# A third V copy moved to ScalarE, an O^T copy moved to VectorE, and filler matmuls re-spread around PV and the fold

## The chip, the cores and the metric

The kernel is one program on one core of a Trainium2 chip. The metric is the device time of one execution in microseconds. A program that computes the forward value and all gradients is launched once; nothing is computed outside it.

## The reference, cut to what matters

The reference computes a block with two residual branches, its output, and the gradients of everything. The part that the change touches is the forward of branch A, a recurrent attention over 64 segments of 32 tokens:

```python
for s in range(n_seg):                       # 64 segments
    h = concat([mem, x[s*32:(s+1)*32]])      # 8 memory rows + 32 rows = 40 rows of 512
    q, k, v = h @ Wq, h @ Wk, h @ Wv         # 32 heads of 128
    p = softmax(mask(q @ k.T * scale))       # per head, 40 x 40
    o = (p @ v) @ Wo                         # 40 x 512
    mem = o[:8]                              # the next segment needs this
    outs.append(o[8:])
```

A segment cannot start before the first 8 output rows of the segment before it, so the 64 segments are a serial chain. The rest (the modulation row, the gated branch B, the backward of both) comes after it and is not touched.

## The kernel before, in words

The method `phase2` runs the 64 segments one after the other. Four segments share one tile of 128 rows of x; `s4 = s % 4` is a segment's place in its tile, and four segments in a row are called a group here. A segment's own passes take 32 of its 40 rows: the 8 of `mem` and the first 24 of x. The last 8 rows of x are known beforehand and are projected for all four segments of the next tile at once ("b rows", "tail rows"), as filler work on TensorE that is spread over the group.

The order on every engine is the order in which the code is written: `pin` chains each instruction to the one before it on its engine. Tile inserts the semaphores, and it lets two engines read one PSUM tile only one after the other. `psp` is a pool of 5 PSUM banks for nearly everything, `pst` one of 3 for the scores.

One segment, in order of TensorE:

1. K and Q projections (`proj`, line 255, four passes of 16 matmuls in four 32-column strips), each half copied out by VectorE or ScalarE into `RA`.
2. V's first chunk (`v_chunk(s, 0)`, line 650), `turns` (transposes of K and Q, line 763), V's second chunk. A V chunk uses three of the four column strips for the segment; the fourth strip carries V's tail rows for the next tile (`RBv`). Chunks are 4, 4 and 3 head groups wide (`VCH`). `self.evac("act" or "dve", ...)` picks ScalarE (line 61) or VectorE (line 63) for the copy out.
3. Scores (`st_exp`, line 773) onto a mask that was put into the score banks one segment earlier by `mask_mm` (line 717, three matmuls: 480, 480 and 360 columns), exp on ScalarE (line 775), V's third chunk.
4. PV in three parts: `den` (line 779, the row sums), `pv` (line 799), `recip` on VectorE (line 784), `ost` (scaling by 1/sum: parts 0 and 2 on VectorE, line 811; part 1 on ScalarE as four instructions, line 808). `pv(2)` and `den(2)` write the bank `or2` that the first `recip` reads, so they wait for it.
5. `ott(0..2)`: transposes of the scaled rows (line 791) and their copies to `OT`, parts 0 and 2 by ScalarE, part 1 by VectorE. `outproj` (line 223) starts with part 0.
6. The fold: `split_pair` takes the output apart into a high half (ScalarE, line 230) and a low half (VectorE, line 232), `sum_pair` adds the strips on TensorE (line 240), and ScalarE copies 8 rows into the next segment's `hT` (line 936). The next K projection waits for that copy.

Around these stand fillers: the b rows' K and Q passes under `fill(s4, "f1")` between `outproj` and the fold, their transposes under `fill(s4, "turn")`, a part of the modulation row once per group (`mod_rest`, line 200) in front of `ott(0)`, the masks of the next segment before and between the `ott`, `p1` (normalising a later tile of x), and in the last segment of a group the tail's own output projection (`tail.chunk`, line 215) in two pieces around the fold.

Of the kernel before, what the change touches and what calls it, by code (L numbers as in the profile page):

```python
# [40 lines left out]
class K:  # L41
# [395 lines left out]
    def phase2(self):  # L437
        nc, tc, cfg, io = self.nc, self.tc, self.cfg, self.io
        D, DC, H, E, L, M, T, G, NS = cfg.D, cfg.DC, cfg.H, cfg.E, cfg.L, cfg.M, cfg.T, cfg.G, cfg.NS
        GW = 128  # L440
        NP = 3
# [9 lines left out]
        with ExitStack() as ctx:  # L451
# [39 lines left out]
            NT = cfg.NT  # L491
# [45 lines left out]
            sb2 = ctx.enter_context(tc.tile_pool(name="p2s2", bufs=2))  # L537
# [17 lines left out]
            def part3(t, pi):  # L555
                return t[:, pi * PW:min((pi + 1) * PW, G * GW)].rearrange("p (g x) -> p g x", x=GW)
# [48 lines left out]
            def b_pieces(t):  # L605

                bt = btails[t] = {}
                RBt = RB

                def proj_b(x, a, n, eng):  # L610
                    hb = hxs[t][1]
                    self.col_pass(psp, Ws[x], 0, lambda c: hb[:, c, :, :].rearrange("p s q -> p (s q)"), RBt[x], eng, steps=(a, n))
                    if a + n == 8:
                        rows_out(RBt[x], DR[x], t * nseg_t, nseg_t)

                def turn_b(x):
# [12 lines left out]
                T_ = lambda x: (lambda: turn_b(x))  # L629
                return {(0, "f1"): [P("k", 0, 4, "dve"), P("k", 4, 2, "act")], (1, "f1"): [P("k", 6, 2, "dve"), P("q", 0, 4, "act")],  # L630
                        (2, "turn"): [T_("k")], (2, "f1"): [P("q", 4, 4, "dve")], (3, "turn"): [T_("q")]}

            evacs = []

# [2 lines left out]
                    evacs.pop(0)()  # L637

            first = b_pieces(0)
            first = [f for k in ((0, "f1"), (1, "f1"), (2, "f1"), (2, "turn"), (3, "turn")) for f in first[k]]  # L640
            firsts = {"k": [first[i] for i in (0, 1, 2, 5)] + [evac_turned], "q": [first[i] for i in (3, 4, 6)] + [evac_turned]}
            slots = {}

            VCH = ((0, 4), (4, 4), (8, 3))

            def v_mm(ps, j, c, lhsT, hl, a, n):

                wc = Wv[:, c, :].rearrange("p (h e) -> p h e", e=E)
                n = min(n, (H - hl + 2) // 3 - a)
                nc.tensor.matmul(ps[32 * j:32 * j + 32, 0:n * E], lhsT=lhsT, rhs=wc[:, 3 * a + hl:3 * (a + n - 1) + hl + 1:3, :],  # L650
                                 start=(c == 0), stop=(c == DC - 1), tile_position=(0, 32 * j))

            def v_evac(eng, dst, ps, a, n):

                m = n if a + n < G else n - 1
                self.evac(eng, dst[0:96, a * E:(a + m) * E], ps[0:96, 0:m * E])
                if m < n:
                    self.evac(eng, dst[0:64, (a + m) * E:(a + n) * E], ps[0:64, m * E:n * E])

            def hb_rows(t):  # L660
                return lambda c: hxs[t][1][:, c, :, :].rearrange("p s q -> p (s q)")
# [10 lines left out]
            def v_chunk(s, k):  # L672

                t, s4 = s // nseg_t, s % nseg_t
                a, n = VCH[k]
                tail_of = None
                if t + 1 < NT:
                    tail_of = (s4,) + VCH[k] if s4 < 3 and k < 2 else (k,) + VCH[2] if s4 == 3 else None
                ps = psp.tile([128, 512], F32, name="pass_ps", tag="p")
                hT = get_ht(s)  # L680
                for c in range(DC):
                    for j in range(3):
                        v_mm(ps, j, c, hT[:, c, :], j, a, n)
                    if tail_of:
                        v_mm(ps, 3, c, hb_rows(t + 1)(c), *tail_of)
                if k > 0:
                    v_evac("dve", Vsts[s % 2], ps, a, n)
                if tail_of:
                    hl, ta, tn = tail_of
                    tn = min(tn, (H - hl + 2) // 3 - ta)  # L690
                    self.evac(("act", "dve", "dve")[k], RBv[(t + 1) % 2][32 * hl:32 * hl + 32, ta * E:(ta + tn) * E],
                              ps[96:128, 0:tn * E])
                if k == 0:
                    v_evac("dve", Vsts[s % 2], ps, a, n)

            def fill(s4, where):
                for f in slots.pop((s4, where), []):
                    f()

            norms = []  # L700
            mod_r = []
            mod_at = sorted([4 * i + 4 for i in range(4 * DC - 1)] + [7])
# [10 lines left out]
            def mask_mm(pi):  # L713

                n = min(PG, G - pi * PG)
                ps = masked[pi] = pst.tile([128, PG, GW], F32, name="st_ps", tag="st")
                nc.tensor.matmul(ps[:, 0:n, 0:120], lhsT=self.ident[:, :], rhs=maskT[:, 0:n, :], start=True, stop=False,
                                 skip_group_check=True)
# [19 lines left out]
            for s in range(NS):  # L738
                s4 = s % nseg_t
                if s4 == 0:  # L740
                    if s > 0:
                        p1(s // nseg_t + P1_AHEAD, 0)
                    slots = b_pieces(s // nseg_t + 1) if s + nseg_t < NS else {}
# [50 lines left out]
                def pv(pi, or_ps=None):  # L794
                    or_ps = or_ps or ps_f32("or_ps")
                    n = min(PG, G - pi * PG)
                    for j in range(n):
                        g = pi * PG + j
                        nc.tensor.matmul(or_ps[:, j, :], lhsT=ET[:, g * GW:(g + 1) * GW], rhs=Vst[:, g * GW:(g + 1) * GW],
                                         start=True, stop=True)  # L800
                    return or_ps
# [11 lines left out]

                def ott(pi):
                    ps, n = transposes_part(Ost, pi, m=120)
                    self.evac("dve" if pi == 1 else "act", part3(OT, pi)[:, 0:n, 0:120], ps)

                def outproj():
                    ps = psp.tile([128, 256], F32, name="at_ps", tag="p")
# [67 lines left out]
                early = s4 == 0 and len(self.later) > 1  # L887
                if early:
                    self.pop_later()
                pv(2, or2)  # L890
                den(2, or2)
                recip(2, 3, or2)
                ost(2, or2, "dve")
                more = list(range(NP)) if s + 1 < NS else []
                turned = bool(slots.get((s4, "turn"))) or bool(mod_r)
                mod_row = mod_r.pop()() if mod_r else None
                if s + 1 in mod_at:
                    load, products = self.mod_rest(psp, sb2, mod_at.index(s + 1))
                    load()
                    mod_r.append(products)  # L900
                fill(s4, "turn")
                if s4 == 3:
                    turned = True
                if more and not turned:
                    mask_mm(more.pop(0))
                    mask_mm(more.pop(0))
                ott(0)
                if len(more) > 1:
                    mask_mm(more.pop(0))
                ott(1)  # L910
                if len(more) > 1:
                    mask_mm(more.pop(0))
                ott(2)
                if more:
                    mask_mm(more.pop(0))
                if not early:
                    self.pop_later()
                self.pop_later()
                nc.sync.dma_start(self.OSR[s], gl3(Ost))
                at_ps = outproj()  # L920
                evac_turned()
                if mod_row:
                    mod_row()
                if s4 < 3:
                    p1(s // nseg_t + P1_AHEAD, s4 + 1)
                if s + 1 < NS:
# [7 lines left out]
                ft = self.sum_pair(psp, parts, "at", "p")  # L934
                if hT_next is not None:
                    nc.scalar.activation(hT_next[:, :, 0:M], ft[:, :, 0:M], AF.Copy)  # L936
                if s4 == 3:
                    tail.chunk()
                tail.split()
# [14 lines left out]
            for pi in range(NP):  # L954
                ps, n = transposes_part(ET, pi)
# [4 lines left out]
            for pi in range(NP):  # L960
                ps, n = transposes_part(Vst, pi)
# [1238 lines left out]
```

## Time and profile before

| | |
|---|---|
| times of three runs | 3095.11, 3099.77, 3098.11 us; median 3098.11 us |
| the profiled execution | 3101.05 us; its span 3099.3 us; mean granted TensorE clock 0.991 |
| TensorE busy | 2981.1 us, 96% of the span |
| VectorE, ScalarE, GpSimd busy | 53%, 41%, 39% |
| DMA, mean over the span | 227 GB/s |
| the 64 segments | from 18.3 us to about 1005 us |

Four segments from the middle start (first K matmul, line 255, in the timeline) at 529.25, 544.22, 559.13 and 573.62 us, and the next one at 589.15: they take 14.97, 14.91, 14.49 and 15.53 us for s4 = 0, 1, 2, 3, together 59.90 us. In the timeline a row gives the start, the time to the last end, engine, line, operation, tiles and count, and in brackets the idle time of that engine before the row with what ended it. A matmul row's time includes the way through the array, so consecutive rows overlap; what counts for TensorE's speed is the distance between starts.

### The profile page before, as it was taken

What the parts mean: (1) busy time and instruction counts of PE and PEld (TensorE: products, weight loads), DVE (VectorE), ACT (ScalarE), POOL (GpSimd) and SP (SyncE); (2) the same over time, 40 slices, a digit from 0 to 9 for tenths busy, and PEclk for the clock granted to TensorE, in tenths of its full rate; (3) what the DMA queues carried; (4) which work ended last, traced back from release to release, by engine and by line L of the source; (5) the groups of instructions that cost most, each with busy time, mean ns of one, the idle gap of its engine ahead of it and who ended that gap; (6) DMA issues with size and microseconds to landing.
All of it is one profiled execution on the core that took longest, in us unless ns stands there. A gap on an engine that the chain in (4) does not pass through costs nothing. (4 is left out here: it accounts for less than half of the span.)

```text
span 3099.3 us, 106370 instructions
## 1 busy us (share of the span) xinstructions
PE 2981.1 (96%) x44229; PEld 1849.8 (60%) x44229; DVE 1644.9 (53%) x3874; ACT 1257.6 (41%) x3036; POOL 1215.9 (39%) x2640
## 2 busy tenths in 40 slices
PE   6999999999999799989999999999999999999999
PEld 3666666666666444445567777777777754445454
DVE  5666666666665788743255555555555542322321
ACT  2555555555554444412145555555555530111011
POOL 2454545555444222211244444444444432333322
PEclk8999999999999899999999999999999999999999
DMA  9777777777777799997689999999999998666574
GB/s 298 212 212 203 204 207 205 204 207 211 203 200 232 210 226 237 212 278 254 202 210 249 243 242 250 252 243 247 244 242 252 244 276 279 199 198 219 191 235 148
DMA packets 839319, 703.53 MB, mean 227 GB/s; under 512 B 539730, under 2 KB 711794, under 8 KB 837940
## 3 DMA queue, kind: packets, MB, share of 16 engines
q1 hardware_dynamic: 713668, 486.69, 60.5%
q0 software_dynamic: 54512, 148.63, 15.2%
q10 hardware_dynamic: 70656, 61.41, 6.3%
q8 instruction: 348, 5.70, 0.8%
q14 instruction: 135, 1.11, 0.1%
HBM read 294.93 MB, written 276.35 MB: 184 GB/s over the span
## 5 line engine op out<-in xcount | busy, mean ns | idle before, releaser
L1990 PE MATMUL gps<-rows,hrows 128*128 128x512 bf16 (+2 forms) x2160 | 417.5, 355 | 0.0
L1990 PEld LDWEIGHTS <-hrows 128*128 128x128 bf16 x2160 | 211.2, 98 | 204.6
L63 DVE CAST ot<-gps 128x512 bf16<-128x512 f32 (+3 forms) x76 | 48.2, 634 | 292.3 <-PE gps L1990 204.6
L1696 POOL COPY dOst<-RAd 96x512 bf16<-96x512 bf16 x128 | 75.4, 613 | 308.3 <-DVE RAd L63 308.3
L255 PEld LDWEIGHTS <-hT 128*32 128x32 bf16 x4096 | 117.2, 97 | 123.6 <-POOL kT L65 14.2
L650 PE MATMUL pass_ps<-Wv,hT 128*32 128x512 bf16 (+2 forms) x2304 | 186.7, 357 | 0.0
L61 ACT ACTIVATE ot<-gps 128x512 bf16<-128x512 f32 (+3 forms) x75 | 41.3, 551 | 354.3 <-PE gps L1990 208.4
L63 DVE CAST Vst<-pass_ps 96x512 bf16<-96x512 f32 (+2 forms) x256 | 126.7, 515 | 108.5 <-ACT RBv L61 92.0
L1994 POOL DMA_DIRECT2D out_dram<-ot x108 | 81.6, 755 | 254.8 <-DVE ot L63 130.6
L945 POOL TENSOR_TENSOR Pst<-Pst,rden 120x1408 bf16<-120x1408 bf16 x63 | 159.6, 2533 | 6.3 <-POOL hT L545 3.8
L255 PE MATMUL pass_ps<-Wk,hT 128*32 128x512 bf16 x2048 | 122.3, 380 | 22.6 <-ACT hT L936 15.3
L61 ACT ACTIVATE dVT<-g_ps 128x480 bf16<-128x480 f32 (+1 forms) x192 | 104.6, 545 | 96.7 <-PE g_ps L1652 96.4
L341 POOL DMA_DIRECT2D AOA<-at_rb x64 | 36.4, 568 | 259.9 <-DVE at_rb L337 259.9
L215 PE MATMUL dh_ps<-WvT,dVT 128*32 128x512 bf16 x2048 | 134.3, 382 | 0.3
L255 PE MATMUL pass_ps<-Wq,hT 128*32 128x512 bf16 x2048 | 124.1, 383 | 6.2 <-DMA Wq<-in_A_Wq_dram 6.2
L728 POOL DMA_DIRECT2D Vst<-RBv x192 | 100.4, 527 | 75.8 <-DVE RBv L63 37.0
L650 PE MATMUL pass_ps<-Wv,hb 128*32 128x512 bf16 (+2 forms) x576 | 129.6, 364 | 0.0
L2004 PE MATMUL gps5o<-WoT,rows 128*128 128x512 bf16 x592 | 128.4, 379 | 1.2 <-DMA rows<-OSR 1.2
L223 PE MATMUL at_ps<-Wo,OT 128*32 128x256 bf16 x4096 | 124.6, 274 | 4.1 <-DMA Wo<-in_A_Wo_dram 4.0
L255 PE MATMUL pass_ps<-WoT,dyT 128*32 128x256 bf16 (+1 forms) x3072 | 122.5, 308 | 0.9 <-ACT dyT L1770 0.9
L223 PE MATMUL dhq_ps<-WqT,dQT 128*32 128x256 bf16 x4096 | 122.9, 273 | 0.0
L215 PE MATMUL dh_ps<-WkT,dKT 128*32 128x512 bf16 x2048 | 122.3, 380 | 0.0
(413 smaller groups left out, 7047.9 us busy)
## 6 DMA issues: line engine op xcount, KB each, us to landing
OSR<-Ost SPq DMA_DIRECT2D x64, 352.0 KB
OT<-OT SPq DMA_DIRECT2D x64, 352.0 KB
VT<-VTr SPq DMA_DIRECT2D x64, 352.0 KB
PS<-Pst SPq DMA_DIRECT2D x64, 352.0 KB
OT_l<-OT SPq DMA_DIRECT2D x64, 352.0 KB
Pst_l<-PS SPq DMA_DIRECT2D x64, 352.0 KB
VT_l<-VT SPq DMA_DIRECT2D x64, 352.0 KB
DVR<-rows_x POOLq DMA_DIRECT2D x64, 352.0 KB, 6.2
```

Source lines behind the costliest of these rows:

```text
L61: return nc.scalar.activation(out, in_, AF.Copy)
L63: return nc.vector.tensor_copy(out, in_)
L215: self.nc.tensor.matmul(ps[32 * j:32 * j + 32, :], lhsT=lhsT, rhs=w, start=(n < 4), stop=(n >= total - 4), tile_position=(0, 32 * j))
L223: nc.tensor.matmul(ps[32 * j:32 * j + 32, :], lhsT=x[k], rhs=w[k][:, 256 * d:256 * d + 256], start=(n == 0), stop=(n == total - 1), tile_p ...
L255: self.nc.tensor.matmul(ps[32 * j:32 * j + 32, :], lhsT=lhs(c), rhs=rhs, start=(c == 0), stop=(c == DC - 1), tile_position=(0, 32 * j))
L650: nc.tensor.matmul(ps[32 * j:32 * j + 32, 0:n * E], lhsT=lhsT, rhs=wc[:, 3 * a + hl:3 * (a + n - 1) + hl + 1:3, :], start=(c == 0), stop=( ...
L728: nc.gpsimd.dma_start(Vst[96 + 8 * j:104 + 8 * j, :], rb[32 * j + o:32 * j + o + 8, :])
L945: nc.gpsimd.tensor_tensor(Pst[0:120, :, :], Pst[0:120, :, :], rden[:, :].unsqueeze(2).to_broadcast([120, G, 128]), op=ALU.mult)
L1696: nc.gpsimd.tensor_copy(dOst[0:96, 512 * hf:512 * hf + 512], RAd[0:96, 512 * hf:512 * hf + 512])
L1990: nc.tensor.matmul(ps[:, 0:ng * E], lhsT=hrows[:, tp_, c * 128:(c + 1) * 128], rhs=rows[:, tp_, 0:ng * E], start=(tp_ == 0), stop=(tp_ == ...
L1994: nc.gpsimd.dma_start(outw[c * 128:(c + 1) * 128, h0:h0 + 3 * (ng - 1) + 1:3, :], ot[:, 0:ng * E].rearrange("p (h e) -> p h e", e=E))
L2004: nc.tensor.matmul(pss[gg][:], lhsT=src[0][:, src[1], gg * E:(gg + 1) * E], rhs=dyrows[:, tp_, :], start=(tp_ == order[0]), stop=(tp_ == o ...
```

## The change

- The copy of V's third chunk goes from VectorE to ScalarE.
- V's tail rows that were spread over all three chunks of the last segment of a group now go with its first two chunks, two per chunk, side by side in the fourth strip of one bank (3 + 1 and 2 + 2 head groups). The third chunk carries none. There are 16 such matmuls per group where there were 12.
- `OT`'s first part is copied by VectorE and its second by ScalarE (before: the other way round).
- One mask matmul stands in front of `pv(2)`, one between `ott(0)` and `ott(1)`, and the third behind the copy to `hT`. Before, two or none stood in front of `ott(0)` and the others between and behind the `ott`.
- The b rows' passes are cut anew: K in two passes of 4 (before 4 + 2 + 2), Q in passes of 2, 4 and 2 (before 4 + 4). Two of the Q passes stand in a new place, `f2`, behind the copy to `hT`.
- The modulation products and the load of their weights stand behind the copy to `hT` too; before they stood in front of `ott(0)`, with the weights' load issued on SyncE's queue before `OSR`'s store.

```diff
-                return {(0, "f1"): [P("k", 0, 4, "dve"), P("k", 4, 2, "act")], (1, "f1"): [P("k", 6, 2, "dve"), P("q", 0, 4, "act")],
-                        (2, "turn"): [T_("k")], (2, "f1"): [P("q", 4, 4, "dve")], (3, "turn"): [T_("q")]}
+                return {(0, "f1"): [P("k", 0, 4, "dve")], (1, "f1"): [P("k", 4, 4, "dve")], (1, "f2"): [P("q", 0, 2, "act")],
+                        (2, "turn"): [T_("k")], (2, "f1"): [P("q", 2, 4, "dve")], (2, "f2"): [P("q", 6, 2, "act")],
+                        (3, "turn"): [T_("q")]}
...
+            VTAILS = {(s4, k): ((s4,) + VCH[k] + (0,),) for s4 in range(3) for k in range(2)}
+            VTAILS[3, 0] = ((0, 8, 3, 0), (1, 8, 1, 3))
+            VTAILS[3, 1] = ((1, 9, 2, 0), (2, 8, 2, 2))
...
-                nc.tensor.matmul(ps[32 * j:32 * j + 32, 0:n * E], lhsT=lhsT, rhs=wc[:, 3 * a + hl:3 * (a + n - 1) + hl + 1:3, :],
-                                 start=(c == 0), stop=(c == DC - 1), tile_position=(0, 32 * j))
+                nc.tensor.matmul(ps[32 * j:32 * j + 32, o * E:(o + n) * E], lhsT=lhsT,
+                                 rhs=wc[:, 3 * a + hl:3 * (a + n - 1) + hl + 1:3, :], start=(c == 0 and o == 0),
+                                 stop=(c == DC - 1), tile_position=(0, 32 * j), skip_group_check=True)
...
                 if k > 0:
-                    v_evac("dve", Vsts[s % 2], ps, a, n)
-                if tail_of:
-                    hl, ta, tn = tail_of
-                    tn = min(tn, (H - hl + 2) // 3 - ta)
-                    self.evac(("act", "dve", "dve")[k], RBv[(t + 1) % 2][32 * hl:32 * hl + 32, ta * E:(ta + tn) * E],
-                              ps[96:128, 0:tn * E])
+                    v_evac(("dve", "act")[k - 1], Vsts[s % 2], ps, a, n)
+                for hl, ta, tn, o in tails_of:
+                    self.evac(("act", "dve")[k], RBv[(t + 1) % 2][32 * hl:32 * hl + 32, ta * E:(ta + tn) * E],
+                              ps[96:128, o * E:(o + tn) * E])
...
-                    self.evac("dve" if pi == 1 else "act", part3(OT, pi)[:, 0:n, 0:120], ps)
+                    self.evac("dve" if pi == 0 else "act", part3(OT, pi)[:, 0:n, 0:120], ps)
...
+                more = list(range(NP)) if s + 1 < NS else []
+                if more:
+                    mask_mm(more.pop(0))
                 pv(2, or2)
                 den(2, or2)
                 recip(2, 3, or2)
                 ost(2, or2, "dve")
-                more = list(range(NP)) if s + 1 < NS else []
-                turned = bool(slots.get((s4, "turn"))) or bool(mod_r)
-                mod_row = mod_r.pop()() if mod_r else None
-                if s + 1 in mod_at:
-                    load, products = self.mod_rest(psp, sb2, mod_at.index(s + 1))
-                    load()
-                    mod_r.append(products)
                 fill(s4, "turn")
-                if s4 == 3:
-                    turned = True
-                if more and not turned:
-                    mask_mm(more.pop(0))
-                    mask_mm(more.pop(0))
                 ott(0)
-                if len(more) > 1:
+                if more:
                     mask_mm(more.pop(0))
                 ott(1)
-                if len(more) > 1:
-                    mask_mm(more.pop(0))
                 ott(2)
-                if more:
-                    mask_mm(more.pop(0))
...
                 if hT_next is not None:
                     nc.scalar.activation(hT_next[:, :, 0:M], ft[:, :, 0:M], AF.Copy)
+                if more:
+                    mask_mm(more.pop(0))
+                fill(s4, "f2")
+                if mod_r:
+                    mod_r.pop()()()
+                if s + 1 in mod_at:
+                    load, products = self.mod_rest(psp, sb2, mod_at.index(s + 1))
+                    load()
+                    mod_r.append(products)
                 if s4 == 3:
                     tail.chunk()
```

More of the change, by code (lines that the diff above doesn't have):

```diff
@@ L639, in phase2, with v_mm @@
             first = b_pieces(0)
-            first = [f for k in ((0, "f1"), (1, "f1"), (2, "f1"), (2, "turn"), (3, "turn")) for f in first[k]]
-            firsts = {"k": [first[i] for i in (0, 1, 2, 5)] + [evac_turned], "q": [first[i] for i in (3, 4, 6)] + [evac_turned]}
+            firsts = {x: [first[k][0] for k in ks] + [evac_turned]
+                      for x, ks in (("k", ((0, "f1"), (1, "f1"), (2, "turn"))),
+                                    ("q", ((1, "f2"), (2, "f1"), (2, "f2"), (3, "turn"))))}
             slots = {}
             VCH = ((0, 4), (4, 4), (8, 3))
-            def v_mm(ps, j, c, lhsT, hl, a, n):
+            VTAILS = {(s4, k): ((s4,) + VCH[k] + (0,),) for s4 in range(3) for k in range(2)}
+            VTAILS[3, 0] = ((0, 8, 3, 0), (1, 8, 1, 3))
+            VTAILS[3, 1] = ((1, 9, 2, 0), (2, 8, 2, 2))
+            def v_mm(ps, j, c, lhsT, hl, a, n, o=0):
                 wc = Wv[:, c, :].rearrange("p (h e) -> p h e", e=E)
                 n = min(n, (H - hl + 2) // 3 - a)
-                nc.tensor.matmul(ps[32 * j:32 * j + 32, 0:n * E], lhsT=lhsT, rhs=wc[:, 3 * a + hl:3 * (a + n - 1) + hl + 1:3, :],
-                                 start=(c == 0), stop=(c == DC - 1), tile_position=(0, 32 * j))
+                nc.tensor.matmul(ps[32 * j:32 * j + 32, o * E:(o + n) * E], lhsT=lhsT,
+                                 rhs=wc[:, 3 * a + hl:3 * (a + n - 1) + hl + 1:3, :], start=(c == 0 and o == 0),
+                                 stop=(c == DC - 1), tile_position=(0, 32 * j), skip_group_check=True)
             def v_evac(eng, dst, ps, a, n):
@@ L675, in v_chunk @@
                 a, n = VCH[k]
-                tail_of = None
-                if t + 1 < NT:
-                    tail_of = (s4,) + VCH[k] if s4 < 3 and k < 2 else (k,) + VCH[2] if s4 == 3 else None
+                tails_of = VTAILS.get((s4, k), ()) if t + 1 < NT else ()
                 ps = psp.tile([128, 512], F32, name="pass_ps", tag="p")
@@ L683, in v_chunk @@
                         v_mm(ps, j, c, hT[:, c, :], j, a, n)
-                    if tail_of:
-                        v_mm(ps, 3, c, hb_rows(t + 1)(c), *tail_of)
+                    for of in tails_of:
+                        v_mm(ps, 3, c, hb_rows(t + 1)(c), *of)
                 if k > 0:
-                    v_evac("dve", Vsts[s % 2], ps, a, n)
-                if tail_of:
-                    hl, ta, tn = tail_of
-                    tn = min(tn, (H - hl + 2) // 3 - ta)
-                    self.evac(("act", "dve", "dve")[k], RBv[(t + 1) % 2][32 * hl:32 * hl + 32, ta * E:(ta + tn) * E],
-                              ps[96:128, 0:tn * E])
+                    v_evac(("dve", "act")[k - 1], Vsts[s % 2], ps, a, n)
+                for hl, ta, tn, o in tails_of:
+                    self.evac(("act", "dve")[k], RBv[(t + 1) % 2][32 * hl:32 * hl + 32, ta * E:(ta + tn) * E],
+                              ps[96:128, o * E:(o + tn) * E])
                 if k == 0:
@@ L921, in phase2 @@
                 evac_turned()
-                if mod_row:
-                    mod_row()
                 if s4 < 3:
```

## The prediction, made before the changed kernel had run

> **What bounds the kernel now.** I read the page first (busy shares, slices), then the sums by window, TensorE's waits, and the timelines of TensorE, VectorE and ScalarE for four segments. The change touches the 64 forward segments, 18 to about 1005 us. The page's first part and the window that covers most of them:
>
> ```profile
> PE 2981.1 (96%) x44229; PEld 1849.8 (60%) x44229; DVE 1644.9 (53%) x3874; ACT 1257.6 (41%) x3036; POOL 1215.9 (39%) x2640
> ...
> 500.00:900.00 400.00, 385.87 (x7518) 255.29 (x7506) 250.06 (x634) 211.44 (x557) 201.47 (x446) 1.00 0.74 206
> ```
>
> In 400 us TensorE is busy 386, at full granted clock (1.00), the others about half; DMA is at 0.74. So the stage is TensorE's work plus the short waits in it. TensorE's waits between 200 and 1200 us name two sites here:
>
> ```profile
> PE pass_ps L255 <- ACT hT L936: 12.1, 26, 0.6
> PE or_ps L799 <- DVE rden L784: 6.4, 13, 0.7
> ```
>
> They understate it, as a matmul's row runs on while the next could have started. Distances between starts tell more. A segment with s4 = 1 (544.22 to 559.13), TensorE's timeline, from PV on:
>
> ```profile
> 552.44 0.24 PE L779 MATMUL or_ps<-ones,ET 128*128 128x1 bf16 x4
> 552.55 0.86 PE L799 MATMUL or_ps<-Vst,ET 128*128 128x128 bf16 x7
> 553.24 0.21 PE L779 MATMUL or_ps<-ones,ET 128*128 128x1 bf16 x3
> 553.32 0.56 PE L717 MATMUL st_ps<-maskT,ident 128*128 128x480 bf16 x2
> 553.81 1.01 PE L791 MATMUL tps<-ident,Ost 120*128 120x120 bf16 x11
> 554.65 0.32 PE L717 MATMUL st_ps<-maskT,ident 128*128 128x360 bf16 x1
> ...
> 555.01 1.93 PE L223 MATMUL at_ps<-Wo,OT 128*32 128x256 bf16 x64
> 556.77 0.61 PE L255 MATMUL pass_ps<-Wk,hb 128*32 128x256 bf16 x16
> 557.21 1.04 PE L255 MATMUL pass_ps<-Wq,hb 128*32 128x512 bf16 x16
> 558.18 0.27 PE L240 MATMUL at_ft<-foldsel,at_hi 128*128 128x32 bf16 x4
> 558.29 0.25 PE L240 MATMUL at_ft<-foldsel,at_lo 128*128 128x32 bf16 x4
> 559.13 0.40 PE L255 MATMUL pass_ps<-Wk,hT 128*32 128x512 bf16 x4 [0.58 <-ACT hT L936]
> ```
>
> Seven PV matmuls at 0.055 (pv(0)'s four take 0.22) need 0.39; they take 0.69, so pv(2) waits 0.31 for the reciprocal. Eleven transposes at 0.053 need 0.58 and take 0.84. From the low fold to the next K pass it is 0.84 where 0.10 is work. With s4 = 3, VectorE copies V's third chunk and a tail before the reciprocal:
>
> ```profile
> 581.62 0.61 DVE L63 CAST Vst<-pass_ps 96x256 bf16<-96x256 f32 x2 [0.17 <-PE pass_ps L650]
> 582.26 0.43 DVE L63 CAST RBv<-pass_ps 32x256 bf16<-32x256 f32 x1
> 582.72 0.21 DVE L784 RECIPROCAL rden<-or_ps 120x8 f32<-120x8 f32 x1
> ```
>
> **Part 1: PV to outproj, s4 = 1, step by step.** The reciprocal starts 0.36 after den(1) starts where VectorE is free (last segment: 1000.33 to 1000.69), so at 552.80 and not 552.84, and ends at 552.99. pv(2) follows 0.05 later, 553.04 (553.08 before); the mask in front of it (0.21) lies wholly in that wait, and den(2) ends at 553.29. V's third copy: ScalarE's exps end at 552.50. Its nearest rows are 128x256 f32 at 0.38 and 128x96 at 0.26, successors starting 0.1 early, so about 552.96: just in time. With 0.37 for the second (a scaled 128x128) it is 0.1 later; with VectorE's own 0.61 nothing changes. I take 0.56 and no cost. Part 0 of the scaled rows: 553.02 to 553.71 (VectorE, 0.69), ott(0) at 553.77. The second mask fills 553.98 to 554.19. ScalarE's part 1 starts 0.17 behind the reciprocal (as before) and takes 1.14, to 554.30, so ott(1) ends at 554.43. Part 2: reciprocal at 553.63, scaling 553.83 to 554.39, ott(2) 554.45 to 554.61. OT's first part, now 0.41 on VectorE right behind part 2: 554.32 to 554.73. (Before, ScalarE took 0.58 for it behind its own part 1, to 554.95, and outproj came at 555.01.) Two small transposes and the switch to 32-column strips (0.09: after such a transpose 0.15 goes by and not 0.06) bring TensorE to 554.81. Outproj: 554.82, gain 0.19. VectorE is now the chain: reciprocal, scaling, reciprocal, scaling, copy.
>
> The other segments by the same rows, offsets from the segment's start: s4 = 2, where the transposes of K's b rows (0.46) hide the wait for part 0: 10.91 to 10.60, gain 0.31. s4 = 0, where a 0.43 copy of the tail's fold stands on VectorE between the two scalings: 11.06 to 10.90, gain 0.16. s4 = 3: the reciprocal goes from 582.72 to 582.16 (0.36 behind den(1) at 581.80), since third copy and tail copy are gone from VectorE in front of it; part 1 is done at 583.66, the copy of hx behind it (0.61, ScalarE) at 584.17. In the built program the small transpose before outproj takes the bank that hx's copy frees, so outproj starts at 584.39, not 585.25: gain 0.86.
>
> The Trainium skill (VectorE: DVE Perf Modes, Specifications) says that ScalarE sits closer to PSUM, which speaks against giving OT's first part to VectorE. The rows say 0.41 on VectorE and 0.58 on ScalarE for the same 128x480; by the rule 0.17 would be lost in three of four segments, some 7 us in all.
>
> **Part 2: the fold, s4 = 1.** Outproj ends 1.76 after its start. The low half's fold can start 1.18 after that (s4 = 2, where one 512-wide pass of 0.97 stands there, shows it), and K follows 0.64 behind it when only the copy to hT is between: 1.83 in all. Before: 2.36, since two passes (1.41) stood in front and ScalarE's 0.60 copy of the second ran ahead of hT's. After: 1.18 + 0.10 (fold) + 0.16 (mask) + 0.09 (switch) + 0.44 (256-wide pass) = 1.97. Gain 0.39. s4 = 0: 2.15 before; after, 1.18 + 0.10 + 0.16 + 0.09 + 0.45 (eight products at 0.056) = 1.98; gain 0.17. s4 = 2: 1.83 before, 1.97 after, a loss of 0.14: more work than wait. s4 = 3: the tail's pieces hid the copy already, so the mask costs its 0.16.
>
> **Part 3: what is moved at no cost.** K's and Q's passes have the same columns in all. VectorE's copies in f1 (0.69) sit behind the low half. The f2 copy (0.38) and the modulation row's (0.25) stand on ScalarE behind hT's, in front of a copy that comes 2 us into the next segment. On SyncE the last Q rows' six stores (0.6 each) and the weights' load come about 0.5 later, ahead of the stores of V^T and P; GpSimd's MODROW store waits at the next segment's start, with the hT copy that is needed 14 us later and the 2.53 us P scaling behind it. No DMA ends a TensorE wait in this stage; if that slack went it would show at exp, 7 us into the segment.
>
> V's tails: with two matmuls in one strip its columns still sum to 512 (384 + 128, 256 + 256), what the other strips stream in 0.215 per step. The third chunk runs strips of 384, 384 and 256 at the widest's 0.163, so unequal strips add nothing: I take 0. If each second part cost its own 0.056 on top, eight per group are 0.45, 6.6 us in all; below zero is excluded, the columns being no fewer. ScalarE copies tails of 0.49 and 0.27 in place of 0.48, which pushes VectorE's Q copies 0.16 later against 0.1 of slack: 0.05 at the scores of s4 = 3. The Trainium skill (TensorE: Matmul & The Clock Gate, Step-by-step) says that matmuls stay in program order; a second part would then hold the next step's three behind it until the first part's 384 columns are through, which is inside the 0.215 and also gives 0.
>
> **The sum.** s4 = 0: 0.16 + 0.17 = 0.33. s4 = 1: 0.19 + 0.39 = 0.58. s4 = 2: 0.31 - 0.14 = 0.17. s4 = 3: 0.86 - 0.16 - 0.05 = 0.65. A group: 1.73 of 59.90 us. Segments 1 to 59 are 14.75 groups, 25.5 us; the last four have no b rows and give about 0.7. Together 26 us. On the profiled execution (3101.05, span 3099.3) that is 3075; it lies 2.9 above the median of three, 3098.1, from which I predict 3072.
>
> **Rivals.** (a) Half of it, 15%: the copy of OT's first part starts later on VectorE than its row's distances say, so outproj keeps its place in s4 = 0 to 2, and the fold and s4 = 3 alone gain: 0.17 + 0.39 - 0.14 + 0.65 = 1.07 a group, 16 us, 3082. For it: the five VectorE steps are back to back, and before there was 0.28 idle in front of its OT copy. Against: those rows show no gaps otherwise.
> (b) Slower, 6%: the same VectorE chain slips far. Each 0.1 on OT's copy costs 0.1 in s4 = 0 to 2, and in s4 = 3 beyond 0.19. Break-even is 3d + (d - 0.19) = 1.73, d = 0.48; at d = 0.7 it is 0.88 a group, 13 us, 3111. For it: ScalarE and VectorE may not read one bank together (VectorE's V copies wait for ScalarE's RBv 1.7 us at most). Against: no bank is shared on this chain.
> (c) The change doesn't bring TensorE closer, as the granted clock falls with fewer pauses, 3%: 0.01 of clock over 930 us is 9 us, break-even 0.97. Against: 1100 to 1300 us runs 200 of 200 us busy at 1.00.
>
> **Numbers.** The forecast's own range: 6.6 for the tails, 0.1 in outproj for three segments of a group (4.5 either way), 0.05 of f2's switch (2): 3065 to 3084. With (a), 3062 to 3088 leaves out 2 in 10. Forecast 74%, (a) 15, (b) 6, (c) 3, unknown 2. A measurement of this kernel can tell about 0.2%, 6 us, from no change. Faster needs under 3092: forecast and (a) nearly whole, 0.87; same 0.06; slower 0.07.
>
> **What would show it.** Groups of 58.2 us; outproj at 10.9, 10.6, 10.6, 10.8 in its segment; no wait for hT; the reciprocal of s4 = 3 at 8.5 and not 9.1; the f2 pass ending in K without a gap. Wrong would be: V's steps of s4 = 3 over 0.215, a new wait for Vst from ScalarE at pv(2), exps that wait for a DMA, a clock below 1.00.

## The result and the profile after

| | before | after |
|---|---|---|
| median of four runs | 3098.77 us (3095.11 to 3099.77) | 3074.64 us (3071.52 to 3075.99) |
| ratio, 95% interval | | 0.9923 [0.9906, 0.9940] |
| profiled execution, its span | 3101.05, 3099.3 us | 3071.52, 3069.7 us |
| segments s4 = 0, 1, 2, 3 (medians of the middle 56) | 14.97, 14.91, 14.49, 15.53 | 14.44, 14.52, 14.30, 15.03 |
| a group of four | 59.90 us | 58.29 us |

The changed kernel is 24.1 us faster; 3072 was predicted. First the page's first part and the window over the middle of the forward:

```profile
PE 2972.8 (97%) x44289; PEld 1859.2 (61%) x44289; DVE 1604.4 (52%) x3746; ACT 1285.6 (42%) x3179; POOL 1212.6 (40%) x2640
...
500.00:900.00 400.00, 395.26 (x7767) 265.70 (x7755) 236.82 (x589) 228.27 (x630) 211.17 (x471) 1.00 0.81 211
```

TensorE's busy time in the window goes from 386 to 395 of 400 us at the same clock: the pauses were taken out and more segments fit in. VectorE gave up about 40 us over the span and ScalarE took 28.

The next fence is TensorE's waits between 200 and 1200 us, the largest first (total, times, longest). The 12.1 us for `hT` and the 6.4 us for `rden` are down to 0.2 and 0.4; what is new is a short wait of `ott(0)` for VectorE's scaled part 0.

```profile
PE mm L1111 <- DMA hdT<-h: 12.3, 1, 12.3
PE tps L794 <- DVE Ost L814: 8.9, 41, 0.3
PE tp L1027 <- ACT Wq L61: 3.8, 7, 1.5
```

And TensorE's timeline of a segment with s4 = 1 (470.78 to 485.30), from the masks on:

```profile
479.49 0.37 PE L720 MATMUL st_ps<-maskT,ident 128*128 128x480 bf16 x1
479.87 0.33 PE L802 MATMUL or_ps<-Vst,ET 128*128 128x128 bf16 x3
480.03 0.22 PE L782 MATMUL or_ps<-ones,ET 128*128 128x1 bf16 x3
480.50 0.38 PE L794 MATMUL tps<-ident,Ost 120*128 120x120 bf16 x4 [0.25 <-DVE Ost L814]
480.72 0.37 PE L720 MATMUL st_ps<-maskT,ident 128*128 128x480 bf16 x1
480.93 0.58 PE L794 MATMUL tps<-ident,Ost 120*128 120x120 bf16 x7
...
481.56 1.93 PE L223 MATMUL at_ps<-Wo,OT 128*32 128x256 bf16 x64
483.31 1.04 PE L255 MATMUL pass_ps<-Wk,hb 128*32 128x512 bf16 x16
484.28 0.27 PE L240 MATMUL at_ft<-foldsel,at_hi 128*128 128x32 bf16 x4
484.50 0.27 PE L240 MATMUL at_ft<-foldsel,at_lo 128*128 128x32 bf16 x4
484.61 0.31 PE L720 MATMUL st_ps<-maskT,ident 128*128 128x360 bf16 x1
484.86 0.62 PE L255 MATMUL pass_ps<-Wq,hb 128*32 128x256 bf16 x16
485.30 1.04 PE L255 MATMUL pass_ps<-Wk,hT 128*32 128x512 bf16 x16
```

Mask and `f2` pass fill the time behind the fold, and K follows without a gap. From outproj to K it is 3.74, where it was 4.12 before. This segment starts 0.15 "late" inside itself, though: its scores come at 6.55 and not at 6.40. The border to the segment before it shows why:

```profile
470.49 0.51 PE L200 MATMUL mod_ps<-wmod_r,sc_keep 128*32 128x128 bf16 x6
470.78 0.40 PE L255 MATMUL pass_ps<-Wk,hT 128*32 128x512 bf16 x3
470.83 0.28 PE L200 MATMUL mod_ps<-wmod_r,sc_keep 128*32 128x128 bf16 x2
470.94 1.89 PE L255 MATMUL pass_ps<-Wk,hT 128*32 128x512 bf16 x29
```

The eight modulation products sit in one column strip. K's first matmuls in the three other strips start at 470.78 while two products are still to come, and the fourth strip follows 0.16 behind. So 0.15 of the segment with s4 = 0 is counted in the next one; below it is put back.

In the last segment of a group (here the one that starts at 499.97) the scores come at 6.49 and not at 6.40, and it takes 0.84 from the first of their eleven matmuls to the pass behind them, where it took 0.68. VectorE's and ScalarE's timelines there:

```profile
505.36 0.69 DVE L63 CAST Vst<-pass_ps 96x512 bf16<-96x512 f32 x1 [1.88 <-ACT RBv L61]
505.97 0.94 DVE L63 COPY qT<-turn_ps 128x384 bf16<-128x384 bf16 x5
...
507.53 0.89 DVE L63 CAST RBv<-pass_ps 32x256 bf16<-32x256 f32 x2
508.74 0.21 DVE L787 RECIPROCAL rden<-or_ps 120x8 f32<-120x8 f32 x1 [0.32 <-PE or_ps L782]
```

```profile
504.55 0.78 ACT L61 ACTIVATE RBv<-pass_ps 32x384 bf16<-32x384 f32 x2 [0.30 <-PE pass_ps L656]
505.35 1.27 ACT L61 ACTIVATE kT<-turn_ps 128x384 bf16<-128x384 bf16 x5
...
508.18 0.54 ACT L61 ACTIVATE Vst<-pass_ps 96x256 bf16<-96x256 f32 x2
509.12 1.14 ACT L811 ACTIVATE Ost<-or_ps,rden 120x128 bf16<-120x128 f32 x4 [0.39 <-PE p1tp L418]
```

The same place in the kernel before, in the segment from 573.62:

```profile
578.19 0.48 ACT L61 ACTIVATE RBv<-pass_ps 32x384 bf16<-32x384 f32 x1 [0.29 <-PE pass_ps L650]
578.71 0.69 DVE L63 CAST Vst<-pass_ps 96x512 bf16<-96x512 f32 x1 [1.58 <-DMA QST<-RBq]
```

The two tail copies on ScalarE (0.78) end before VectorE begins the copy of V's first chunk, which lies in the same bank. It begins at 5.39 of the segment, 5.09 before the change, and the Q and K copies that the scores need come 0.23 to 0.30 later. The reciprocal is at 8.77, not at the predicted 8.54 (9.10 before).

### The profile page after: what moved, and what is told of

The parts are those of the page before. It is cut to its first block, busy times and chain, and to the rows that moved or that the text cites. A ratio compares the mean times of both kernels' runs of the same rounds, so it can differ in the third digit from the quotient of the medians.

```text
span 3069.7 us, 106628 instructions
## 1 busy us (share of the span) xinstructions
PE 2972.8 (97%) x44289; PEld 1859.2 (61%) x44289; DVE 1604.4 (52%) x3746; ACT 1285.6 (42%) x3179; POOL 1212.6 (40%) x2640
## 5 line engine op out<-in xcount | busy, mean ns | idle before, releaser
L255 PEld LDWEIGHTS <-hT 128*32 128x32 bf16 x4096 | 125.1, 97 | 95.8 <-DMA Wq<-in_A_Wq_dram 6.2
L942 POOL TENSOR_TENSOR Pst<-Pst,rden 120x1408 bf16<-120x1408 bf16 x63 | 159.8, 2537 | 39.1 <-issue 23.3
L63 DVE CAST Vst<-pass_ps 96x512 bf16<-96x512 f32 x128 | 87.3, 682 | 107.4 <-ACT RBv L61 97.7
L223 PEld LDWEIGHTS <-dQT 128*32 128x32 bf16 x4096 | 109.7, 97 | 15.7
```

The costliest lines, as they stand in the source:

```text
L63: return nc.vector.tensor_copy(out, in_)
L223: nc.tensor.matmul(ps[32 * j:32 * j + 32, :], lhsT=x[k], rhs=w[k][:, 256 * d:256 * d + 256], start=(n == 0), stop=(n == total - 1), tile_p ...
L255: self.nc.tensor.matmul(ps[32 * j:32 * j + 32, :], lhsT=lhs(c), rhs=rhs, start=(c == 0), stop=(c == DC - 1), tile_position=(0, 32 * j))
L942: nc.gpsimd.tensor_tensor(Pst[0:120, :, :], Pst[0:120, :, :], rden[:, :].unsqueeze(2).to_broadcast([120, G, 128]), op=ALU.mult)
```

## The experiments

The theory: the gain is in three independent places, each worth what its rows say. They are the third V copy off VectorE, the copy of `OT`'s first part off ScalarE, and fillers put into waits of TensorE, above all behind the fold. The miss is one term in s4 = 3, ScalarE's second tail copy. The rivals: the fold alone or the outproj alone carries the gain; VectorE's longer chain costs something unseen; the two-part tails themselves cost.

The measure is the length of segments in each profiled execution (medians of 56 segments, repeated to 0.01 us). The whole time is coarser: in these profiles the first segment alone takes from 42.7 to 46.2 us and what follows the first K matmul of the last segment from 2098 to 2111 us. The kernels ran in three groups, each beside runs of the kernel before on the same chip, so across groups the ratios are compared. The groups are c_after, c_before, e3p and e4p; e1p, e2p, e5p and b1p_masks_early; and the two at the end.

| kernel | median us (range) | ratio to before | s4 = 0, 1, 2, 3 | group |
|---|---|---|---|---|
| c_before | 3097.20 (3093.07 to 3100.03) | 0.9985 [0.9976, 0.9995] | 14.97 14.90 14.48 15.52 | 59.87 |
| c_after | 3073.92 (3072.77 to 3076.00) | 0.9912 [0.9897, 0.9927] | 14.44 14.52 14.30 15.03 | 58.28 |
| e3p_fold_back | 3086.09 (3083.38 to 3087.47) | 0.9949 [0.9933, 0.9965] | 14.91 14.88 14.30 14.91 | 59.00 |
| e4p_tails_three | 3071.13 (3069.39 to 3074.92) | 0.9900 [0.9883, 0.9918] | 14.44 14.52 14.30 14.98 | 58.23 |
| e1p_v3_vector | 3074.98 (3071.59 to 3078.54) | 0.9930 [0.9914, 0.9947] | 14.48 14.54 14.32 15.27 | 58.62 |
| e2p_ot_back | 3081.92 (3079.05 to 3085.76) | 0.9950 [0.9935, 0.9965] | 14.44 14.56 14.44 15.35 | 58.79 |
| e5p_tail_late | 3070.73 (3069.42 to 3071.11) | 0.9912 [0.9897, 0.9927] | 14.44 14.52 14.30 14.81 | 58.07 |
| b1p_masks_early | 3063.52 (3061.81 to 3064.10) | 0.9889 [0.9874, 0.9903] | 14.44 14.20 14.16 14.70 | 57.50 |
| c_after_again | 3077.11 (3075.32 to 3078.11) | 0.9924 [0.9911, 0.9938] | 14.44 14.52 14.30 15.03 | 58.28 |
| b1p_again | 3063.99 (3061.93 to 3066.79) | 0.9885 [0.9871, 0.9898] | 14.44 14.20 14.16 14.70 | 57.49 |

### The two controls

```diff
-                nc.sync.dma_start(VTr[:], Vst[:, :], transpose=True)
+                nc.sync.dma_start(VTr[:], gl3(Vst))
```

Eight such DMAs are changed in the kernel after (c_after) and in the one before (c_before), and in all kernels below. They copy the tiles without transposing them, so the gradients that need the transposed values are left out.

> The kernel after, with its eight transposing DMAs replaced by plain copies of the same tiles (the gradients that need the transposed values are left out; order, engines and sizes of the forward are unchanged). It is the control for the kernels below. Theory: the forward's groups of four segments do not rest on these DMAs, so they stay at 58.28 us (within 0.1). Rival: the stores of V^T and P on SyncE's queue held something in the forward back; then a group is shorter by over 0.3 us.

> The kernel before with the same eight DMAs as plain copies. Theory: groups of 59.9 us, so it is 1.6 us per group, 24 to 26 us in all, slower than the control. Rival: part of the gain came through the transposing DMAs; then the difference per group is under 1.3 us.

Groups of 58.28 and 59.87 us, as in the unchanged kernels (58.29 and 59.90): the length of the forward's segments does not hang on these DMAs. The difference is 1.59 us per group and 23.3 us in all, with the rival's bound at 1.3. The kernels below are set against c_after.

### The fold's fillers back

```diff
-                return {(0, "f1"): [P("k", 0, 4, "dve")], (1, "f1"): [P("k", 4, 4, "dve")], (1, "f2"): [P("q", 0, 2, "act")],
-                        (2, "turn"): [T_("k")], (2, "f1"): [P("q", 2, 4, "dve")], (2, "f2"): [P("q", 6, 2, "act")],
-                        (3, "turn"): [T_("q")]}
+                return {(0, "f1"): [P("k", 0, 4, "dve"), P("k", 4, 2, "act")], (1, "f1"): [P("k", 6, 2, "dve"), P("q", 0, 4, "act")],
+                        (2, "turn"): [T_("k")], (2, "f1"): [P("q", 4, 4, "dve")], (3, "turn"): [T_("q")]}
...
                 ott(2)
+                if more:
+                    mask_mm(more.pop(0))
...
-                if more:
-                    mask_mm(more.pop(0))
-                fill(s4, "f2")
```

The modulation products go back in front of `ott(0)` as well.

> The control, but the fillers around the fold as in the kernel before: K's b rows 4+2+2, Q's 4+4, no pass, mask or modulation product behind the copy to hT; the modulation products in front of ott(0); the third mask behind ott(2). Theory: the low half's fold to K takes 2.15, 2.36 and 1.83 us again in s4 = 0, 1, 2 (after: 1.94, 1.99 and 1.94 with the border counted in the segment that ends); the mask adds 0.15 in front of outproj in s4 = 0 to 2; s4 = 3 gains 0.16 and loses 0.04. Sum 0.7 to 0.8 us per group, 11 us slower than the control. Rival (the fold is no bound, the gain is all before outproj): within 2 us of the control.

0.72 us per group and 12.2 us in all were lost, as the theory had it. TensorE's timeline of a segment with s4 = 1 has the old picture back, the wait for ScalarE's copy to `hT`:

```profile
545.95 0.61 PE L255 MATMUL pass_ps<-Wk,hb 128*32 128x256 bf16 x16
546.38 1.04 PE L255 MATMUL pass_ps<-Wq,hb 128*32 128x512 bf16 x16
547.35 0.27 PE L240 MATMUL at_ft<-foldsel,at_hi 128*128 128x32 bf16 x4
547.47 0.25 PE L240 MATMUL at_ft<-foldsel,at_lo 128*128 128x32 bf16 x4
548.30 1.05 PE L255 MATMUL pass_ps<-Wk,hT 128*32 128x512 bf16 x16 [0.58 <-ACT hT L931]
```

It splits in two. From outproj to K it takes 3.91, 4.11, 3.59 and 3.90 in s4 = 0 to 3, and in the control 3.74, 3.75, 3.75 and 4.06 (the border's 0.15 put back, the third mask's own 0.16 included): together 0.21. The rest is the third mask, 0.15 in front of outproj in each of s4 = 0 to 2 and 0.04 in s4 = 3. So of the 0.72, two thirds come from masks that no longer stand in front of outproj, and only a third from the fold proper. With the 0.87 that this kernel still has over c_before, the rival (the fold carries nothing) and the other extreme (it carries all) are both out.

### The third V copy back to VectorE

```diff
-                    v_evac(("dve", "act")[k - 1], Vsts[s % 2], ps, a, n)
+                    v_evac("dve", Vsts[s % 2], ps, a, n)
```

> The control, but V's third chunk is copied by VectorE as in the kernel before (its tail rows stay with the first two chunks). Theory: the copy matters only where VectorE is busy when the chunk is done. In s4 = 0 to 2 VectorE is free for it and the reciprocal comes at most 0.05 us later; in s4 = 3 VectorE copies two tails (0.89) until 8.40, so the copy (0.61) ends near 8.95 and the reciprocal moves from 8.77 to about 8.95: 0.15 to 0.35 us per group, 3 to 5 us in all. Rival: the third copy was the main load in front of the reciprocal; then the reciprocal goes back to 9.1 in s4 = 3, comes 0.1 to 0.2 later in the others, and the group is longer by 0.6 us or more, 10 us in all.

0.34 us per group: 0.04, 0.03, 0.03 and 0.24. In s4 = 3 (from 561.50) VectorE's timeline shows the copy in the reciprocal's way, which starts at 9.02:

```profile
569.06 0.89 DVE L63 CAST RBv<-pass_ps 32x256 bf16<-32x256 f32 x2
569.98 0.61 DVE L63 CAST Vst<-pass_ps 96x256 bf16<-96x256 f32 x2
570.52 0.19 DVE L787 RECIPROCAL rden<-or_ps 120x8 f32<-120x8 f32 x1
```

That is the theory's upper end; the rival's 0.6 is excluded. The whole time rose by only 1.1 us in medians, but by 0.0018 (5.6 us) in the ratios, whose intervals overlap; 14.75 groups make 5.0. The copy is not quite free on ScalarE either: `pv(2)` comes 0.07 to 0.08 earlier here in s4 = 1 and 2 (9.01 and 8.85 for 9.09 and 8.92). That doesn't reach outproj, which comes 0.03 later.

### OT's first part back to ScalarE

```diff
-                    self.evac("dve" if pi == 0 else "act", part3(OT, pi)[:, 0:n, 0:120], ps)
+                    self.evac("dve" if pi == 1 else "act", part3(OT, pi)[:, 0:n, 0:120], ps)
```

> The control, but OT's first part is copied by ScalarE and its second by VectorE, as in the kernel before; the third stays on ScalarE. Theory: the first part (0.57 on ScalarE) then stands behind part 1's scaling, and in s4 = 3 behind the copy of hx as well; outproj comes 0, 0.05, 0.1 and 0.35 later in s4 = 0, 1, 2, 3: 0.5 us per group, 7 us slower. Rival (a price of the copy on VectorE that the rows do not show, VectorE's chain being the late one): outproj stays or comes earlier, and the time is the same or lower.

Outproj comes 0.00, 0.05, 0.14 and 0.32 later, 0.51 us per group or 7.5 us over 14.75 groups; the whole time rose by 8.0 us in medians and by 0.0038 (11.8 us) in the ratios, whose intervals lie apart. VectorE's longer chain shows no hidden price. ScalarE's timeline in s4 = 3 shows the first part queued behind part 1 and `hx` (the turned rows of a later tile, which `p1` prepares), and TensorE's the wait that follows from it:

```profile
572.55 1.14 ACT L811 ACTIVATE Ost<-or_ps,rden 120x128 bf16<-120x128 f32 x4 [0.40 <-PE p1tp L418]
573.57 0.61 ACT L420 ACTIVATE hx<-p1tp 128x512 bf16<-128x512 bf16 x1
574.04 0.96 ACT L61 ACTIVATE OT<-tps 128x480 bf16<-128x480 bf16 x2
```

```profile
574.70 0.84 PE L223 MATMUL at_ps<-Wo,OT 128*32 128x256 bf16 x24 [0.25 <-ACT OT L61]
```

Two things count, and not the same in each segment. In s4 = 3 it is the queue: the copy starts at 10.64 on ScalarE and at 10.32 on VectorE in the control. In s4 = 1 and 2 it is the copy's own length, 0.57 on ScalarE and 0.40 on VectorE: it starts no later on ScalarE (10.19 and 10.07) than on VectorE (10.26 and 10.10), but ends 0.10 and 0.15 later. In s4 = 0 the copy ends before outproj could start on either engine (10.69 and 10.78), as `ott(2)` comes at 10.53 in both, and the exchange is worth nothing. These are bf16 rows; for f32 rows the order is the other way, 0.60 for 128x512 on ScalarE and 0.69 on VectorE (`RA1k` in the profile after).

### V's tails over three chunks again

```diff
-            VTAILS[3, 0] = ((0, 8, 3, 0), (1, 8, 1, 3))
-            VTAILS[3, 1] = ((1, 9, 2, 0), (2, 8, 2, 2))
+            for k in range(3):
+                VTAILS[3, k] = ((k, 8, 3 if k < 2 else 2, 0),)
...
-                    self.evac(("act", "dve")[k], RBv[(t + 1) % 2][32 * hl:32 * hl + 32, ta * E:(ta + tn) * E],
+                    self.evac(("act", "dve", "act")[k], RBv[(t + 1) % 2][32 * hl:32 * hl + 32, ta * E:(ta + tn) * E],
```

> The control, but V's tail rows in the last segment of a group go with all three chunks again (one matmul per step, 12 per group instead of 16); the third chunk's tail is copied by ScalarE behind the third V copy. Theory: V's second copy no longer waits for two tail copies on ScalarE (0.78), so the scores of s4 = 3 start at 6.40 and not 6.49 and take 0.68 and not 0.84; outproj of s4 = 3 at about 10.7 and not 10.97. A gain of 0.2 to 0.25 us per group, 3 to 4 us in all. Rival: ScalarE's longer work behind the third chunk (0.27 to 0.3 more) delays part 1 and hx's copy and outproj goes towards 11.3; then it is 5 us or more slower.

Both halves of the argument were true at once, so neither forecast held. The scores are back at 6.39 and 0.68 long, `pv(2)` comes at 8.92 and not at 9.17, `ott(0)` at 9.61 and not at 9.86. Then 0.20 of the 0.25 is lost at `ott(1)`, which comes at 10.29 and not at 10.34. ScalarE's timeline (segment from 558.97) shows where:

```profile
567.10 0.54 ACT L61 ACTIVATE Vst<-pass_ps 96x256 bf16<-96x256 f32 x2
567.67 0.38 ACT L61 ACTIVATE RBv<-pass_ps 32x256 bf16<-32x256 f32 x1
568.07 1.14 ACT L811 ACTIVATE Ost<-or_ps,rden 120x128 bf16<-120x128 f32 x4
```

The third chunk's tail copy now stands in front of part 1, which starts at 9.10 instead of 8.90 (0.17 behind the reciprocal's end at 8.73). A group is 0.05 shorter, where 0.20 to 0.25 was expected. V's matmul steps keep their 0.215 with one tail matmul or two (with two, in the profile after, they start at 503.43, 503.64, 503.86 and 504.07), so the second tail matmuls are free.

### The second tail copy later on ScalarE

```diff
+                for of in tails_of[:1 if k == 0 else 2]:
+                    tail_out(*of)
                 if k == 0:
                     v_evac("dve", Vsts[s % 2], ps, a, n)
+                    for of in tails_of[1:]:
+                        late_tail.append((tail_out, of))
...
                 turns()
+                while late_tail:
+                    f, of = late_tail.pop()
+                    f(*of)
```

> The control, but in the last segment of a group ScalarE's second tail copy of V's first chunk (0.30) is issued behind its copies of K's turned columns. Theory: VectorE's copy of the first chunk waits for one tail copy and not for two (5.09 instead of 5.39), so the scores of s4 = 3 start at 6.40 and take 0.68, and part 1 is not pushed as it was with three chunks of tails, where the third chunk's tail copy took the gain back. Outproj of s4 = 3 at 10.73 instead of 10.97: 0.24 us per group, 3.5 us faster. Rival: the late copy pushes the exps, or the bank that it holds is missing for a later tile; then the scores start at 6.40 but PV comes no earlier, and the group stays at 58.28.

A group is 0.21 shorter, all of it in s4 = 3. In the segment from 557.24 VectorE's first V copy is back at 5.07 and the reciprocal at 8.54:

```profile
562.31 0.69 DVE L63 CAST Vst<-pass_ps 96x512 bf16<-96x512 f32 x1 [1.56 <-ACT RBv L61]
...
565.78 0.21 DVE L794 RECIPROCAL rden<-or_ps 120x8 f32<-120x8 f32 x1 [0.37 <-PE or_ps L789]
```

```profile
563.69 0.27 ACT L61 ACTIVATE RBv<-pass_ps 32x128 bf16<-32x128 f32 x1
```

The scores come at 6.42 and outproj at 10.75. One copy of 0.27, moved by 1.4 us on an engine that is busy 230 of 400 us in this stretch, gives the missing term back; the rival (exps pushed, a bank missing) is not seen. The whole time is too coarse to show it: 3.2 us less than the control in medians, and the same ratio, 0.9912 in both.

### No mask behind the fold

```diff
                 if more:
                     mask_mm(more.pop(0))
+                    if s4 < 3:
+                        mask_mm(more.pop(0))
                 pv(2, or2)
...
                 ott(2)
+                if more:
+                    mask_mm(more.pop(0))
...
-                if more:
-                    mask_mm(more.pop(0))
                 fill(s4, "f2")
```

> The control with the late tail copy of the run before, and with no mask behind the copy to hT: in s4 = 0 to 2 two masks stand in front of pv(2), which waits 0.17 longer than one mask lasts; in s4 = 3 the third stands behind ott(2), in front of a transpose that waits 0.12 for its bank. Theory: with the mask gone, K follows the low fold by its bound of 0.64 in s4 = 1 and 2 (0.80 now), the modulation products of s4 = 0 end before the next segment's K and no longer 0.15 inside it, and s4 = 3 saves 0.14 in the fold for 0.04 in front of outproj. Together 0.15 + 0.16 + 0.16 + 0.10 and the tail copy's 0.24: 0.8 us per group, 12 us faster than the control. Rival: the second mask is not covered, pv(2) comes 0.1 to 0.15 later in s4 = 0 to 2, and 0.4 us per group is left.

0.78 us per group under the control: 0.31 in s4 = 1 (0.15 of the border and the rest from the fold), 0.14 in s4 = 2, 0.33 in s4 = 3 (0.21 of it from the tail copy). In TensorE's timeline of a segment with s4 = 1 two masks now lie in front of `pv(2)`, which keeps its place (8.96, and 8.94 in the control with the border put back), and K follows the low fold by 0.65:

```profile
532.74 0.57 PE L727 MATMUL st_ps<-maskT,ident 128*128 128x480 bf16 x2
533.14 0.33 PE L809 MATMUL or_ps<-Vst,ET 128*128 128x128 bf16 x3
...
537.74 0.27 PE L240 MATMUL at_ft<-foldsel,at_lo 128*128 128x32 bf16 x4
537.94 0.62 PE L255 MATMUL pass_ps<-Wq,hb 128*32 128x256 bf16 x16
538.39 0.40 PE L255 MATMUL pass_ps<-Wk,hT 128*32 128x512 bf16 x4
```

In s4 = 0 the second mask isn't covered and `pv(2)` comes 0.21 later (9.16), but `ott(0)`, which waits for part 0, stays at 9.57. As the two kernels had run in different groups, where their ratios to the kernel before overlap (0.9912 and 0.9889), both were run again side by side:

> The control once more, on the same chip as the next kernel, so that the two can be set against each other directly. Theory and rival alike: about 3074 us, groups of 58.28.

> The kernel with the late tail copy and no mask behind the copy to hT once more. Theory: 0.78 us per group, 14.75 groups, so 11 to 12 us under the control on the same chip. Rival: the shorter groups leave the rest of the program later (its DMAs start in a fuller queue), and only some 5 us are left.

3063.99 against 3077.11 us, 13.1 us apart, with ranges that don't touch. So this order beats both controls: 0.21 of its 0.78 per group is the tail copy's, the other 0.57 the masks'. It was run in the controls' form, with the plain DMAs, and not with the transposing ones.

## Why the prediction was right, point by point

The two columns are the gains in us; before outproj they are differences of its place in the segment, behind it the differences from outproj to the next K, with the border's 0.15 put back into s4 = 0.

| step | predicted | measured |
|---|---|---|
| s4 = 0, to outproj and behind it | 0.16, 0.17 | 0.21, 0.17 |
| s4 = 1 | 0.19, 0.39 | 0.17, 0.36 |
| s4 = 2 | 0.31, -0.14 | 0.35, -0.16 |
| s4 = 3 | 0.86 - 0.05, -0.16 | 0.66, -0.16 |
| a group | 1.73 | 1.60 |

- **VectorE's chain.** In s4 = 1, after the border's 0.15, `ott(0)`, `ott(2)` and outproj were put at 9.70, 10.38 and 10.75 and came at 9.72, 10.40 and 10.78. `OT`'s first part starts at 10.26 right behind part 2, as worked out. So rival (a), a late copy, fell, and with it (b); the run with the copy back on ScalarE measured its worth, 0.51 per group.
- **The fold.** All four terms held to 0.03, the two losses among them. In s4 = 0 the products did not end before K but ran into it, which the prediction had not seen; it changes where 0.15 is counted, not the sum.
- **V's third copy.** "Just in time" and "no cost" held at outproj. `pv(2)` comes 0.12 later than worked out, and 0.07 to 0.08 of that goes with the copy on ScalarE; the rest stays open. It was named as a sign of being wrong; it appeared and is hidden behind `ott(0)`'s wait for part 0.
- **The tails' matmuls.** The 0 for the second matmuls was right; the bound of 6.6 us was not needed.
- **The mis-sized term.** The prediction puts "0.16 later against 0.1 of slack: 0.05" for ScalarE's second tail copy. It does not say where 0.16 comes from; its two rows (0.49 and 0.27) make 0.28 more than the one of before, and an overlap of about 0.1, which it counts for other neighbours on ScalarE, would explain it. They do not overlap: they take 0.78 together, 0.30 more than the one. VectorE's V copy, which shares their bank, moved by those 0.30, and the scores ended 0.24 later. The run with the second copy issued later gives back 0.21 per group, 3.1 us over 14.75 groups, and the reciprocal at the predicted place. The term is 0.16 (at outproj) to 0.19 (at the scores) short; smaller ones of both signs bring the group's miss to 0.13. The profile before could have told it: the copy behind `RBv`'s 32x512 starts 0.02 after its end in all 45 cases, where V's third pair in the profile after (0.39 and 0.27) overlaps by 0.13. Why these copies don't overlap stays open.

```profile
533.82 0.59 ACT L61 ACTIVATE RBv<-pass_ps 32x512 bf16<-32x512 f32 x1 [0.29 <-PE pass_ps L650]
534.44 1.27 ACT L61 ACTIVATE kT<-turn_ps 128x384 bf16<-128x384 bf16 x5
```

- **The clock** stayed at 1.00 in the window: rival (c) fell. No exp waits for a DMA.
- **The sum.** 14.75 groups at 1.61 make 23.7 us of the 24.1 measured. (The forecast's own upper bound comes to 3085 from its terms, and not to 3084; nothing hangs on it.) The parts nearly add up: taking back the V copy (0.34), the `OT` copy (0.51) and the fillers (0.72) one at a time and taking off the tails' 0.05 gives 1.52 of the control's 1.59. The mask in front of `pv(2)`, which every kernel set against the control kept, was not taken back alone.

The Trainium skill (PSUM — Partial Sum Buffer, Terms) says that different quadrants of one bank may be accessed by two engines at the same time. The V copy that waited reads partitions 0 to 95 and the tail copies 96 to 127, so by that page the 0.30 would be the price of the order that Tile writes down for one tile and not of the chip; no run here shows it, as in none of them the two engines read the bank at the same time.

## What to carry to other kernels

Cost a second small copy at its full duration plus what the bank's next reader waits for, not at its share of an engine that is half idle; then look for a gap in that engine's queue behind the critical reader. See from rows of the same copy whether its neighbours overlap. A filler is free only where the wait around it, or one behind it on the path, is longer than it, so measure each wait as a distance between starts against the work in it, and place fillers by the waits: in s4 = 0 to 2 three masks in two waits took less time than three in three places. To find what a moved step is worth, put back one step at a time and compare stage lengths, which here repeat to 0.01 us where the whole time scatters by several.

## What the runs showed of the hardware that was not expected

Matmuls in different column strips do not start in the order in which they are written. In the profile after, three K matmuls start 0.05 and 0.11 us ahead of two products that were written before them, in another strip. In the run with three chunks of tails, the tail strip, which streams 384 columns every 0.163 us, runs ahead of the other strips' 0.215: its fourth matmul starts at 3.95 of the segment and the three of that step, written before it, at 4.10:

```profile
562.92 0.33 PE L656 MATMUL pass_ps<-Wv,hb 128*32 128x384 bf16 x1
563.07 0.39 PE L656 MATMUL pass_ps<-Wv,hT 128*32 128x512 bf16 x3
```

The Trainium skill (TensorE: Matmul & The Clock Gate, The mechanism) says that matmuls start and end in program order; the measured starts differ, and the ends are modelled in these profiles. For this case it means that a narrow strip's matmuls don't hold up the wide ones, and that the products that run into the next K pass delay one of its strips, by 0.16; the scores behind it come 0.15 later.
